# Softmax exponentials of a windowed attention: one instruction per group or one per head, and their place in the first block

## Chip, core and metric

The kernel runs on one core of a Trainium2 chip. The metric is the device time of one execution in microseconds (us). Engines: PE (TensorE) multiplies matrices, with its weight loads shown apart as PEld; DVE (VectorE) and ACT (ScalarE) do elementwise work; POOL (GpSimd) a little of it; SP (SyncE) issues the DMAs. An engine takes its instructions in the order in which they are written.

## What is computed

A windowed attention with 8 memory keys, then two MLPs with different gates, all in float32 from outside:

```python
for c in range(nc):                        # chunks of 32 queries, 16 keys to the left, 8 to the right
    k_full = np.concatenate([mem_k, k_ctx], axis=2)
    v_full = np.concatenate([mem_v, v_ctx], axis=2)
    scores = scale * np.matmul(q_c, k_full.transpose(0, 1, 3, 2))
    scores = scores - np.max(scores, axis=-1, keepdims=True)
    a = np.exp(scores)
    a = a / (np.sum(a, axis=-1, keepdims=True) + 1e-09)
    out[:, :, c_start:c_end] = np.matmul(a, v_full)
x = out as 3072 tokens x 512               # 4 batches x 768, 8 heads x 64
h = x @ w_in;  g = h - np.tanh(h);  x = g @ w_out          # first MLP, d_ff 2048
h = x @ w_in2; g = piecewise quadratic gate of h; x = g @ w_out2
```

## The kernel before

**Attention.** 24 groups `t` of 4 chunks each hold 128 queries, 8 heads and a window of 64 keys, so a group's scores are a 128 x 512 tile: per query row 8 heads of 64 scores. A group runs through these steps, each of which is a function:
- `att_scores` (L320): 128 small matmuls write the scores into one PSUM pair of banks, `a`.
- `att_max` (L338, L340): DVE takes each head's maximum from PSUM (one reduction), then subtracts it in two instructions that write the SBUF tile `e`.
- `att_exp` (L350): ACT takes the exponential of the whole of `e` in place, one 128 x 512 instruction.
- `att_sum` (L354 to L356): DVE sums each head's exponentials, adds 1e-9 and takes reciprocals.
- `att_transpose` (L362): four PE transposes of `e` into PSUM; `att_at` (L367): ACT copies them out; `att_values` (L376): 128 small matmuls; `att_norm` (L386): DVE multiplies by the reciprocals; `att_x` (L396): four PE transposes; `att_xh` and `att_xl` (L402, L407): ACT and DVE split the result in a high and a low part, the input `xh`, `xl` of the first MLP.

**First MLP.** Six blocks of 512 tokens (four groups each), 16 steps a block. Step `s`: `hidden(s)` (L472) is 12 matmuls into one of two PSUM banks `h`; `gate(s)` has an ACT tanh (L482) and a DVE subtraction (L483), called the gate end here; 16 steps later `output` (L507) multiplies. Weights are rounded on the way: `round_act` (L133 `raw`, L136 `stage`, ACT), `round_mag` and `round_sign` (L142, L143, L151, DVE; L156, POOL), then split in two parts `whi` (L168, ACT) and `wlo` (L175, DVE).

**Order.** Everything is written out by hand. The start runs the groups 0 to 3 one after the other: each pass `j` is scores, maximum, exponential, transposes, copy, values, norm, transposes, split, and PE's gaps are filled with matmuls on zeros (`warm`, L941). In the start ACT's `raw` (L133) stands between the exponential and the copy `at`. Then a loop over steps `i` runs, in this order, lists of events: `before`, `rounds` (weight rounding), then `hidden(i + 1)`, `gate(i + 1)`, then `behind`, then `output`. The groups 4 to 8 are spread over the steps 0, 3, 6, 9, 12 of block 0, where there is no `output` yet; the groups 9 to 23 come every fourth step. For a group at step `i` scores and maximum stand in `behind` of step `i`, exponential and sum in `behind` of `i + 1`, so behind the tanh of `hidden(i + 2)`; the transposes (`slot_b`) follow `hidden(i + 2)` for groups up to 8, and stand behind `hidden(i + 3)` for later ones. Up to group 7 the transposes write a PSUM pair of their own; from group 8 on (`t > 2 * PER - 1`, L434) they write the pair in which the scores stood. The second MLP follows from about 577 us on and has no part in the change.

Of the kernel before, what the change touches and what calls it, by code (L numbers as in the profile page):

```python
# [8 lines left out]
F32 = mybir.dt.float32  # L9
# [4 lines left out]
AF = mybir.ActivationFunctionType  # L14
ALU = mybir.AluOpType
AX = mybir.AxisListType
# [12 lines left out]
WIN = NMEM + LEFT + CHUNK + SEEN  # L29
# [9 lines left out]
PER = 4  # L39
# [34 lines left out]
def tile_memory_attention_two_mlps(  # L74
# [9 lines left out]
    nc = tc.nc  # L84
# [7 lines left out]
    att = ctx.enter_context(tc.tile_pool(name="att", bufs=2))  # L92
# [7 lines left out]
    def slot(tag, name, dtype=F32):  # L100
        return slots.tile([128, 512], dtype, tag=tag, name=name)
# [62 lines left out]
    def split_weights_hi(s, which):  # L164
        phase, b, fc = steps[s]
        r = raw_t[phase, which, fc]
        hi = slot(f"whi{which}_{s % (W1O if which else 2)}", f"whi{which}_{s}", F32R)
        nc.scalar.activation(out=hi, in_=r, func=AF.Copy)  # L168
        split_t[s, which] = hi

    def split_weights_lo(s, which):
        phase, b, fc = steps[s]
        r, hi = raw_t[phase, which, fc], split_t[s, which]
        lo = slot(f"wlo{which}_{s % (W1O if which else 2)}", f"wlo{which}_{s}", F32R)
        nc.vector.tensor_tensor(out=lo, in0=r, in1=hi.bitcast(F32), op=ALU.subtract)  # L175
        split_t[s, which] = hi, lo
# [8 lines left out]
    def w1o_store(s):  # L185
        for i, t in enumerate(split_t[s, 1]):
            nc.sync.dma_start(out=w1o_d[steps[s][2]][:, i, :], in_=t.bitcast(F32))

    def w1o_load(s):
        if s < NS:  # L190
            t = [slot(f"w{w}1_{s % W1O}", f"w{w}1_{s}", F32R) for w in ("hi", "lo")]
            for i in range(2):
                nc.sync.dma_start(out=t[i].bitcast(F32), in_=w1o_d[steps[s][2]][:, i, :])
            split_t[s, 1] = t
# [60 lines left out]
    st = {}  # L255
# [54 lines left out]
    scale = 1.0 / float(D) ** 0.5  # L310
# [17 lines left out]
    def att_max(t):  # L328

        e = slots.tile([128, 4, 2, WIN], F32, tag=f"e{t % 2}", name=f"e{t}")  # L330
        mx = att.tile([128, 2, NPAIR], F32, tag="mx", name=f"mx{t}")
        s = st[t]["sp"]

        if t % GPB == 0:
            nc.vector.memset(s[:CHUNK, :, :, NMEM:NMEM + LEFT], NEG)
        if t % GPB == GPB - 1:
            nc.vector.memset(s[128 - CHUNK:, :, :, WIN - SEEN:], NEG)
        nc.vector.tensor_reduce(out=mx, in_=s, op=ALU.max, axis=AX.X)  # L338
        for hh in range(2):
            nc.vector.tensor_tensor(  # L340
                out=e.rearrange("p (b c) u k -> p c u b k", c=2)[:, hh],
                in0=s[:, hh].rearrange("p (u b) k -> p u b k", u=2),
                in1=mx[:, hh].rearrange("p (u b) -> p u b", u=2)[:, :, :, None].to_broadcast([128, 2, 2, WIN]),
                op=ALU.subtract,
            )
        st[t]["e"] = e

    def att_exp(t):
        e = st[t]["e"]
        nc.scalar.activation(out=e, in_=e, func=AF.Exp, scale=scale)  # L350

    def att_sum(t):
        r = att.tile([128, 4, 2], F32, tag="r", name=f"r{t}")
        nc.vector.tensor_reduce(out=r, in_=st[t]["e"], op=ALU.add, axis=AX.X)  # L354
        nc.vector.tensor_scalar(out=r, in0=r, scalar1=1e-9, scalar2=None, op0=ALU.add)
        nc.vector.reciprocal(out=r, in_=r)  # L356
        st[t]["r"] = r

    def att_transpose(t, p):
        e = st[t]["e"].rearrange("p g u k -> p g (u k)")  # L360
# [56 lines left out]
    def slot_s(t):  # L417
        if t < NG:
            att_scores(t, st_pair.pop(t))
            att_max(t)  # L420
# [7 lines left out]
    def slot_exp(t):  # L428
        att_exp(t)
        att_sum(t)  # L430
# [18 lines left out]
    def x_tiles(phase, b):  # L449
        if (phase, b) not in x_t:  # L450
            x_t[phase, b] = tuple(
                xsp.tile([128, KC, N], F32R, tag=f"x{w}{b % 2}", name=f"x{w}_{b}") for w in "hl"
            )
        return x_t[phase, b]
# [7 lines left out]
    def hidden(s, n0=0, n1=N, parts=range(3)):  # L462
        phase, b, fc = steps[s]
        xh, xl = x_tiles(phase, b)
        hi, lo = split_t[s, 0]
        if s not in h_t:
            h_t[s] = ps_h.tile([128, 512], F32, tag="h", name=f"h{s}")[:, :N]
        hp = h_t[s][:, n0:n1]
        for j in parts:
            w, x = ((hi, xh), (hi, xl), (lo, xh))[j]  # L470
            for kc in range(KC):
                nc.tensor.matmul(  # L472
                    hp, w[:, kc * 128:(kc + 1) * 128], x[:, kc, n0:n1],
                    start=j == 0 and kc == 0, stop=j == 2 and kc == KC - 1,
                )

    def gate(s):
        phase, b, fc = steps[s]
        hp = h_t[s]
        g = slot(f"g{fc}", f"g{s}")  # L480
        g_t[s] = g
        nc.scalar.activation(out=g, in_=hp, func=AF.Tanh)  # L482
        nc.vector.tensor_tensor(out=g, in0=hp, in1=g, op=ALU.subtract)  # L483
        h_t.pop(s)

    def split_g(s):
        hi, lo = slot(f"ghi{s % GSETS}", f"ghi{s}", F32R), slot(f"glo{s % GSETS}", f"glo{s}", F32R)
        split_to(g_t[s], hi, lo)
        g_t[s] = hi, lo
# [350 lines left out]
    for n, p in enumerate(PAIRS[PREP_FIRST:]):  # L840
        f = [
            (prep_act, *p), (prep_rest, *p, 0), (prep_rest, *p, 1), (prep_sums, *p),
            (prep_split, *p, 0), (prep_split, *p, 1), (prep_split, *p, 2), (prep_split, *p, 3),
        ]
# [26 lines left out]
        w1o_load(s + W1O)  # L871


    before, rounds, behind = {}, {}, {}

    def at_step(events, i, f, *args):
        assert i >= 0
        events.setdefault(int(i), []).append((i, f, args))


    for t in range(PER, NG + 1):
        k = t - PER
        i = SPACE_A[0] * min(k, PER) + SPACE_A[1] * max(0, k - PER)

        at_step(behind, max(0, i - 1 + 0.3) if k <= PER else i, slot_v, t)
        at_step(behind, max(0, i - 1 + 0.4) if k <= PER else i + 0.2, slot_norm, t)
        at_step(behind, i + 0.1, slot_s, t)
        if t < NG:
            at_step(behind, i + 1, slot_exp, t)

        at_step(before if k <= PER else behind, i + 2, slot_b, t)
        at_step(before, i + 1.01, att_load, t + 2, True, False)
        if t - 1 >= PER:
            at_step(before, (i if k <= PER else i + 1) + 0.02, att_load, t + 1, False, True)
    at_step(before, 0.5, att_load, PER + 1)
    for w in range(2):
        for fc in range(FC):
            p = fc - EARLY + w * (FC + 2)
# [6 lines left out]
    for n, pair in enumerate(PAIRS):  # L905
        p = int(PREP + PREP_EVERY * n)
# [41 lines left out]
    for j in range(PER):  # L948
        w = 0, 0, j
        pool, tag = ((ps_a, "a"), (ps_acc, "acc0"))[j % 2]  # L950
# [11 lines left out]
        else:  # L962
            warm(KEEP["s"], t_ps)
        att_max(j)
        att_exp(j)
        round_act(*w, 0)
        if 1 <= j <= 2:
            split_weights_lo(j - 1, 0)
        att_sum(j)
        att_transpose(j, t_ps)  # L970
        att_at(j)
# [29 lines left out]
    def run(events, i):  # L1001
        for _, f, args in sorted(events.pop(i, []), key=lambda e: e[0]):
            f(*args)

    for i in range(-1, NS - 1):
        o = i - LAG
        if 0 <= i and i + 2 < NS:
            split_weights_hi(i + 2, 0)
            split_weights_lo(i + 2, 0)
        if 0 <= o + 1:  # L1010
            split_g(o + 1)
            if o + 1 < FC:
                split_weights_hi(o + 1, 1)
                split_weights_lo(o + 1, 1)
        if 0 <= o < FC:
            w1o_store(o)
        if o + W1O - 2 >= FC:
            w1o_load(o + W1O - 2)
        run(before, i)
        run(rounds, i)  # L1020
        hidden(i + 1, EARLY_N if i + 1 < 2 else 0)
        gate(i + 1)
        run(behind, i)
        if o >= 0:
            output(o)
# [11 lines left out]
    for e in plan:  # L1037
# [6 lines left out]
        if e[0] == "P" and e[1] == 0 and e[3] in (1, 4, 2, 7):  # L1044
# [2 lines left out]
            events += 1  # L1047
            if events == 8 * (len(PAIRS) - PREP_FIRST) + 2:
                spare.extend(f"prep{i}" for i in range(9))
    assert not before and not rounds and not behind  # L1050


# [46 lines left out]
```

## Time and profile before

| | |
|---|---|
| median of 3 runs | 1085.6 us (1085.06 to 1085.8) |
| the profiled execution | 1086.91 us |
| its span, first to last instruction | 1085.1 us |
| PE busy | 1065.2 us, 98% |
| DVE / ACT busy | 794.2 us, 73% / 614.7 us, 57% |
| PE busy from 0 to 43 us (the start) | 31.53 of 43 us |
| PE busy from 43 to 110 us (block 0) | 62.71 of 67 us |
| PE busy from 110 to 580 us (blocks 1 to 5) | 470.00 of 470 us |
| granted PE clock over the span | 0.998 of full speed |

One core has one span, and its last instruction ends the time. PE is busy nearly always, so a change in ACT's or DVE's work shows in the time only where PE waits for it, and the rows by stretch say where PE has gaps. A clock of 1 is 2.4 GHz, 0.50 is 1.2 GHz.

### The profile page before, as it was taken

To read this page: it belongs to the slowest core of one execution; us is meant where nothing else is said; L and a number is where in the kernel's file an instruction comes from. 1 tells how busy PE (TensorE), PEld (TensorE's weight loads), DVE (VectorE), ACT (ScalarE), POOL (GpSimd) and SP (SyncE) were. 2 spreads that over 40 slices of the span, in tenths; PEclk is the share of its full clock that TensorE was granted. 3 is DMA by queue.
4 is the path that set the end of the run, shared out by engine and by line. 5 is a ranking of instruction groups with operands and counts; after the bars stand their busy time and mean duration, and the time that the engine had idled before them with its cause. 6 is when DMAs were issued, how large, how long until landed. Compare 5 with 4: busy or idle time off the path is not lost.

```text
span 1085.1 us, 20769 instructions
## 1 busy us (share of the span) xinstructions
PE 1065.2 (98%) x7655; PEld 870.1 (80%) x7655; DVE 794.2 (73%) x1397; ACT 614.7 (57%) x1085; POOL 42.5 (4%) x38
## 2 busy tenths in 40 slices
PE   7899999999999999999999999999999999999998
PEld 3677888888888888888888888878888888888886
DVE  4699987787777777868885765698367797467854
ACT  3566665545454544545465645757477766477553
POOL 1132222000000000000000000000000000000000
PEclk9999999999999999999999999999999999999999
DMA  9997885888788788658779875677766777766664
GB/s 213 242 260 208 263 243 166 256 278 255 246 266 274 223 258 261 224 182 271 275 251 325 293 244 170 199 268 221 240 192 194 233 251 226 220 194 194 203 203 146
DMA packets 201316, 253.04 MB, mean 233 GB/s; under 512 B 65024, under 2 KB 114176, under 8 KB 201216
## 3 DMA queue, kind: packets, MB, share of 16 engines
q1 hardware_dynamic: 201216, 251.72, 75.9%
q8 instruction: 61, 1.00, 0.4%
q14 instruction: 39, 0.32, 0.1%
HBM read 201.33 MB, written 50.33 MB: 232 GB/s over the span
## 4 chain that ended last, share of the span: by engine, by line
PE 97%; ACT 1%; DVE 1%; issue 0%; ACTq 0%; DVEq 0%
PE h L472 25%; PE acc L507 24%; PE acc L793 21%; PE qa L706 12%; PE qc L706 6%; PE qb L706 3%; PE a L376 1%; PE a L320 1%; PE start_tx L941 1%; PE b L362 1%; PE b L396 1%; ACT e L350 0%; PE start_a L320 0%; PE start_a L376 0%; PE start_tx L396 0%
## 5 line engine op out<-in xcount | busy, mean ns | idle before, releaser
L482 ACT ACTIVATE g<-h 128x512 f32<-128x512 f32 x96 | 57.3, 597 | 222.6 <-PE h L472 207.6
L793 PE MATMUL acc<-ghi,inG 128*128 128x512 f32 x672 | 183.1, 389 | 0.0
L222 DVE TENSOR_TENSOR glo<-g,ghi 128x512 fp32r<-128x512 f32 x206 | 140.2, 687 | 35.8 <-ACT ghi L221 34.9
L221 ACT ACTIVATE ghi<-g 128x512 fp32r<-128x512 f32 x206 | 127.4, 626 | 46.5 <-PE acc L793 23.7
L793 PEld LDWEIGHTS acc<-ghi,inG 128*128 128x128 f32 x672 | 126.1, 188 | 26.2
L706 PE MATMUL qa<-xc,inP 128*128 128x512 f32 x576 | 140.1, 389 | 0.0
L483 DVE TENSOR_TENSOR g<-h,g 128x512 f32<-128x512 f32 x96 | 66.2, 690 | 82.0 <-ACT g L482 81.2
L706 PEld LDWEIGHTS qa<-xc,inP 128*128 128x128 f32 x576 | 108.1, 188 | 22.4
L507 PE MATMUL acc<-ghi,whi 128*128 128x512 f32 x384 | 109.2, 399 | 0.0
L793 PE MATMUL acc<-glo,inG 128*128 128x512 f32 x336 | 107.2, 390 | 0.4 <-DVE glo L222 0.3
L472 PE MATMUL h<-xl,whi 128*128 128x512 f32 (+2 forms) x392 | 104.5, 388 | 1.6 <-issue 1.6
L507 PE MATMUL acc<-ghi,wlo 128*128 128x512 f32 x384 | 105.7, 390 | 0.0
L507 PE MATMUL acc<-glo,whi 128*128 128x512 f32 x384 | 105.7, 389 | 0.0
L472 PE MATMUL h<-xh,whi 128*128 128x512 f32 (+2 forms) x392 | 105.2, 390 | 0.0
L472 PE MATMUL h<-xh,wlo 128*128 128x512 f32 (+2 forms) x392 | 104.3, 388 | 0.0
L648 ACT ACTIVATE t<-g,half 128x512 f32<-128x512 f32 x72 | 52.2, 725 | 82.2 <-DVE g L644 82.2
L472 PEld LDWEIGHTS h<-xl,whi 128*128 128x128 f32 x392 | 73.4, 189 | 16.9 <-issue 1.9
L472 PEld LDWEIGHTS h<-xh,wlo 128*128 128x128 f32 x392 | 73.5, 189 | 14.7
L507 PEld LDWEIGHTS acc<-ghi,wlo 128*128 128x128 f32 x384 | 72.1, 188 | 15.4
L507 PEld LDWEIGHTS acc<-glo,whi 128*128 128x128 f32 x384 | 72.1, 188 | 15.2
L472 PEld LDWEIGHTS h<-xh,whi 128*128 128x128 f32 x392 | 72.1, 188 | 14.5
L175 DVE TENSOR_TENSOR wlo<-raw,whi 128x512 fp32r<-128x512 f32 x112 | 79.6, 710 | 4.7 <-ACT whi L168 4.7
(108 smaller groups left out, 1522.3 us busy)
## 6 DMA issues: line engine op xcount, KB each, us to landing
inP<-part SPq DMA_DIRECT2D x168, 256.0 KB, 2.9
inG<-part SPq DMA_DIRECT2D x168, 256.0 KB, 2.9
whi<-w1o SPq DMA_DIRECT2D x80, 256.0 KB, 4.3
wlo<-w1o SPq DMA_DIRECT2D x80, 256.0 KB, 4.5
stage<-w_in SPq DMA_DIRECT2D x32, 512.0 KB, 5.4
stage<-w_out SPq DMA_DIRECT2D x32, 512.0 KB, 4.5
part<-preph SPq DMA_DIRECT2D x64, 256.0 KB, 4.4
part<-prepl SPq DMA_DIRECT2D x48, 256.0 KB, 4.3
```

The costliest lines, as they stand in the source:

```text
L175: nc.vector.tensor_tensor(out=lo, in0=r, in1=hi.bitcast(F32), op=ALU.subtract)
L221: nc.scalar.activation(out=hi, in_=src, func=AF.Copy)
L222: nc.vector.tensor_tensor(out=lo, in0=src, in1=hi.bitcast(F32), op=ALU.subtract)
L320: nc.tensor.matmul(sp[j * CHUNK:(j + 1) * CHUNK, hh, pr, :], qt[j][hh * D:(hh + 1) * D, pr, :], kt[j][hh * D:(hh + 1) * D, pr, :], start=T ...
L362: nc.tensor.transpose(p[:, g * GQ:(g + 1) * GQ], e[:, g, :], ident)
L472: nc.tensor.matmul(hp, w[:, kc * 128:(kc + 1) * 128], x[:, kc, n0:n1], start=j == 0 and kc == 0, stop=j == 2 and kc == KC - 1,)
L482: nc.scalar.activation(out=g, in_=hp, func=AF.Tanh)
L483: nc.vector.tensor_tensor(out=g, in0=hp, in1=g, op=ALU.subtract)
L507: nc.tensor.matmul(acc_t[dm], w[:, dm * 128:(dm + 1) * 128], g, start=first and j == 0, stop=last and j == 2,)
L648: nc.scalar.activation(out=t, in_=h, func=AF.Relu, scale=0.5, bias=half)
L706: nc.tensor.matmul(o, w[:, k * 128:(k + 1) * 128], z[k], start=i in (1, 2, 5) and j == 0 and k == 0, stop=j == 2 and k == 1, skip_group_ch ...
L793: nc.tensor.matmul(bank[a][c], w[:, c * 128:(c + 1) * 128], g, start=first and j == 0, stop=last and j == 2, skip_group_check=True,)
```

## The change

- DVE no longer subtracts the maximum. It multiplies the 8 maxima by -scale (one 128 x 8 instruction).
- ACT takes the exponentials from the scores in PSUM, head by head: 8 instructions of 128 x 64 with the negated maximum as a bias operand, each of which also hands out the sum of its exponentials (`accum_out`). In the built program a second short ACT instruction stands behind each of the 8, which writes that sum.
- DVE's sum over `e` is gone; the 1e-9 and the reciprocal stay.
- For the groups 4 to 8 the maximum moves ahead of the gate end of the same step on DVE (a new list `between`), and the exponentials move into `rounds`, ahead of the next tanh on ACT.

```diff
-        for hh in range(2):
-            nc.vector.tensor_tensor(
-                out=e.rearrange("p (b c) u k -> p c u b k", c=2)[:, hh],
-                in0=s[:, hh].rearrange("p (u b) k -> p u b k", u=2),
-                in1=mx[:, hh].rearrange("p (u b) -> p u b", u=2)[:, :, :, None].to_broadcast([128, 2, 2, WIN]),
-                op=ALU.subtract,
-            )
-        st[t]["e"] = e
+        nc.vector.tensor_scalar(out=mx, in0=mx, scalar1=-scale, scalar2=None, op0=ALU.mult)
+        st[t]["e"], st[t]["mx"] = e, mx
 
     def att_exp(t):
-        e = st[t]["e"]
-        nc.scalar.activation(out=e, in_=e, func=AF.Exp, scale=scale)
+        e, mx, s = (st[t][x] for x in ("e", "mx", "sp"))
+        st[t]["r"] = r = att.tile([128, 4, 2], F32, tag="r", name=f"r{t}")
+        for g in range(4):
+            for u in range(2):
+                hh, pr = g % 2, 2 * u + g // 2
+                nc.scalar.activation(
+                    out=e[:, g, u, :], in_=s[:, hh, pr, :], func=AF.Exp, scale=scale,
+                    bias=mx[:, hh, pr:pr + 1], accum_out=r[:, g, u:u + 1],
+                )
...
-        nc.vector.tensor_reduce(out=r, in_=st[t]["e"], op=ALU.add, axis=AX.X)
...
-        at_step(behind, max(0, i - 1 + 0.3) if k <= PER else i, slot_v, t)
+        at_step(behind if k else between, max(0, i - 1 + 0.3) if k <= PER else i, slot_v, t)
...
-        at_step(behind, i + 0.1, slot_s, t)
+        at_step(between if k <= PER else behind, i + 0.1, slot_s, t)
         if t < NG:
-            at_step(behind, i + 1, slot_exp, t)
+            at_step(rounds if k <= PER else behind, i + 1.5 if k <= PER else i + 1, slot_exp, t)
...
         hidden(i + 1, EARLY_N if i + 1 < 2 else 0)
+        run(between, i)
         gate(i + 1)
         run(behind, i)
```

ACT's queue around group 5's exponentials in block 0, before (`g<-h` is a tanh, `e` the exponentials, `whi`, `raw`, `stage` weight rounding, `at` and `xh` copies from PSUM; the numbers behind a name only tell buffers apart):

```order
L136 ACTIVATE stage_8_780<-stage_8_780 128x512
L482 ACTIVATE g_990<-h_977 128x512
L350 ACTIVATE e_951<-e_951 128x512
L168 ACTIVATE whi_7_998<-raw_7_889 128x512
L402 ACTIVATE xh_1011<-b_1002 128x4x128
L367 ACTIVATE at_1014<-b_1002 128x512
```

And the same place after the change:

```order
L136 ACTIVATE stage_8_799<-stage_8_799 128x512
L348 ACTIVATE e_973,r_1001<-a_875,mx_974 128x64 x8
L481 ACTIVATE g_1025<-h_1012 128x512
L168 ACTIVATE whi_7_1028<-raw_7_914 128x512
L401 ACTIVATE xh_1041<-b_1032 128x4x128
L366 ACTIVATE at_1044<-b_1032 128x512
```

The eight exponentials, which read the scores `a` and the maxima `mx`, moved in front of the tanh; the copies stay behind it.

DVE's queue for the same group, before (`L338` is the maximum, `L340` the subtractions, `L483` a gate end):

```order
L151 SCALAR_TENSOR_TENSOR raw_7_889<-stage_7_702,raw_7_889 128x512
L483 TENSOR_TENSOR g_916<-h_903,g_916 128x512
L337 MEMSET a_850 32x2x4x8
L338 TENSOR_REDUCE mx_952<-a_850 128x8
L340 TENSOR_TENSOR e_951<-a_850,mx_952 128x2x2x64 x2
L175 TENSOR_TENSOR wlo_6_959<-raw_6_825,whi_6_957 128x512
```

And after:

```order
L151 SCALAR_TENSOR_TENSOR raw_7_914<-stage_7_722,raw_7_914 128x512
L337 MEMSET a_875 32x2x4x8
L338 TENSOR_REDUCE mx_974<-a_875 128x8
L339 TENSOR_SCALAR mx_974<-mx_974 128x8
L482 TENSOR_TENSOR g_978<-h_928,g_978 128x512
L175 TENSOR_TENSOR wlo_6_983<-raw_6_850,whi_6_981 128x512
```

The maximum moved in front of the gate end, and a 128 x 8 instruction stands where the two subtractions stood.

PE's queue at the transposes of group 8 with what they wait for, before (a name ending in _49 is the semaphore of that engine):

```order
L396 MATMUL b_1554<-ident,xn_1450 128x128 [waits DVE_49,PE_49]
L396 MATMUL b_1554<-ident,xn_1450 128x128 x3
L362 MATMUL b_1554<-ident,e_1511 128x128 [waits Activation_49]
L362 MATMUL b_1554<-ident,e_1511 128x128 x3
```

And after:

```order
L395 MATMUL b_1599<-ident,xn_1490 128x128 [waits DVE_49,Activation_49]
L395 MATMUL b_1599<-ident,xn_1490 128x128 x3
L361 MATMUL b_1599<-ident,e_1548 128x128 x4
```

The wait for ACT moved from the second four transposes to the first four, which write the banks that the exponentials now read.

## Rows read from the trace of the kernel before

**Rows 1.** The page's first part: busy time, share, instructions of each engine

```profile
PE 1065.2 (98%) x7655; PEld 870.1 (80%) x7655; DVE 794.2 (73%) x1397; ACT 614.7 (57%) x1085; POOL 42.5 (4%) x38
```

**Rows 2.** Who PE waited for: us in total, times, longest us

```profile
PE b L362 <- ACT e L350: 4.3, 5, 1.2
PE start_tx L362 <- ACT e L350: 3.4, 3, 1.4
```

**Rows 3.** Timeline, pass 0 of the start: start us, us, engine line, names [idle before]

```profile
7.68 0.69 DVE L338 TENSOR_REDUCE mx<-start_a 128x8 f32<-128x512 f32 x1
8.41 0.76 DVE L340 TENSOR_TENSOR e<-start_a,mx 128x256 f32<-128x256 f32 x2
9.20 0.63 ACT L350 ACTIVATE e<-e 128x512 f32<-128x512 f32 x1 [6.97 <-DVE e L340]
9.73 0.67 ACT L133 ACTIVATE raw<-stage 128x512 f32<-128x512 f32 x1
...
9.97 0.63 PE L362 MATMUL start_tx<-ident,e 128*128 128x128 f32 x4 [1.39 <-ACT e L350]
...
10.58 0.17 DVE L355 TENSOR_SCALAR r<-r 128x8 f32<-128x8 f32 x1
10.63 0.60 ACT L367 ACTIVATE at<-start_tx 128x512 f32<-128x512 f32 x1 [0.23 <-PE start_tx L362]
...
11.28 0.59 PE L941 MATMUL start_tx<-zeros 128*128 128x512 bf16 x2 [0.69 <-ACT at L367]
```

**Rows 4.** Timeline, pass 3 of the start

```profile
40.80 1.33 PE L472 MATMUL h<-xl,whi 128*128 128x384 f32 x3 [1.61 <-issue]
41.92 1.05 PE L396 MATMUL start_tx<-ident,xn 128*128 128x128 f32 x4
```

**Rows 5.** PE in half-microsecond stretches: us, PE busy (x), PEclk, DMA share, GB/s

```profile
40.50:41.00 0.50, 0.20 (x1) 0.73 0.17 38
...
44.00:44.50 0.50, 0.50 (x6) 0.86 0.27 47
```

**Rows 6.** Timeline, group 4 in block 0

```profile
49.33 0.66 ACT L136 ACTIVATE stage<-stage 128x512 int32<-128x512 uint32 x1
...
52.26 1.17 PE L472 MATMUL h<-xh,whi 128*128 128x512 f32 x4
```

**Rows 7.** Timeline, group 5 in block 0

```profile
59.80 0.69 DVE L151 SCALAR_TENSOR_TENSOR raw<-stage,raw 128x512 int32<-128x512 int32 x1
...
60.62 0.67 ACT L136 ACTIVATE stage<-stage 128x512 int32<-128x512 uint32 x1
...
62.58 0.60 PE L396 MATMUL b<-ident,xn 128*128 128x128 f32 x4
...
64.36 1.17 PE L472 MATMUL h<-xh,whi 128*128 128x512 f32 x4
```

**Rows 8.** Timeline, group 8 in block 0

```profile
95.19 0.86 PE L320 MATMUL a<-k,q 64*32 64x64 f32 x64
...
98.84 0.60 PE L396 MATMUL b<-ident,xn 128*128 128x128 f32 x4
...
100.62 1.17 PE L472 MATMUL h<-xh,whi 128*128 128x512 f32 x4
```

**Rows 9.** Groups of ACT instructions, shapes apart: x count, busy us, mean ns, idle before

```profile
L648 ACT ACTIVATE t<-qa,half 128x512 f32<-128x512 f32 x24 | 16.1, 673 | 0.0
L221 ACT ACTIVATE preph<-raw 128x256 fp32r<-128x256 f32 x32 | 12.3, 408 | 0.0
...
L221 ACT ACTIVATE preph<-raw 128x512 fp32r<-128x512 f32 x8 | 5.0, 623 | 0.0
...
L108 ACT ACTIVATE unused<-half 128x1 f32<-128x1 f32 x1 | 0.2, 203 | 0.0
```

**Rows 10.** Timeline, group 9 in block 1

```profile
118.06 0.63 ACT L350 ACTIVATE e<-e 128x512 f32<-128x512 f32 x1
...
121.51 0.60 PE L396 MATMUL b<-ident,xn 128*128 128x128 f32 x4
```

More of the change, by code (lines that the diff above doesn't have):

```diff
@@ L338, in att_max @@
         nc.vector.tensor_reduce(out=mx, in_=s, op=ALU.max, axis=AX.X)
-        for hh in range(2):
-            nc.vector.tensor_tensor(
-                out=e.rearrange("p (b c) u k -> p c u b k", c=2)[:, hh],
-                in0=s[:, hh].rearrange("p (u b) k -> p u b k", u=2),
-                in1=mx[:, hh].rearrange("p (u b) -> p u b", u=2)[:, :, :, None].to_broadcast([128, 2, 2, WIN]),
-                op=ALU.subtract,
-            )
-        st[t]["e"] = e
-    def att_exp(t):
-        e = st[t]["e"]
-        nc.scalar.activation(out=e, in_=e, func=AF.Exp, scale=scale)
+        nc.vector.tensor_scalar(out=mx, in0=mx, scalar1=-scale, scalar2=None, op0=ALU.mult)
+        st[t]["e"], st[t]["mx"] = e, mx
+    def att_exp(t):
+        e, mx, s = (st[t][x] for x in ("e", "mx", "sp"))
[7 more added lines that the diff above has]
+                )
     def att_sum(t):
-        r = att.tile([128, 4, 2], F32, tag="r", name=f"r{t}")
-        nc.vector.tensor_reduce(out=r, in_=st[t]["e"], op=ALU.add, axis=AX.X)
+        r = st[t]["r"]
         nc.vector.tensor_scalar(out=r, in0=r, scalar1=1e-9, scalar2=None, op0=ALU.add)
         nc.vector.reciprocal(out=r, in_=r)
-        st[t]["r"] = r
     def att_transpose(t, p):
@@ L871, in older @@
         w1o_load(s + W1O)
-    before, rounds, behind = {}, {}, {}
+    before, rounds, between, behind = {}, {}, {}, {}
     def at_step(events, i, f, *args):
@@ L1049, in tile_memory_attention_two_mlps @@
                 spare.extend(f"prep{i}" for i in range(9))
-    assert not before and not rounds and not behind
+    assert not before and not rounds and not between and not behind
 def _windows(np, mem, x):
```

## The prediction

> **What bounds the kernel now.** First the page's busy shares: PE is busy for 98% of the span, DVE and ACT for 73% and 57% [rows 1]. So removing DVE work is worth nothing by itself; only PE's gaps can give or take time. Second, whom PE waits for [rows 2]: the largest item is the exponential. Five transposes in block 0 wait 4.3 us for it together, one for each of the groups 4 to 8, and three in the start wait 3.4 us. The reader is to see that both places of the change lie on a chain that ends in PE, and that 4.3 us is the most that moving block 0's exponentials can give back. Third, the timeline of one pass of the start [rows 3]: maximum, subtractions, exponential, transposes, copy follow each other with gaps of 0.03 to 0.23 us. PE waits 1.39 us in it although zeros are multiplied to fill gaps. The start is a chain of latencies; what is added to a link there is added to the time. In blocks 1 to 5 PE has no gap at all.
>
> **What one group's exponentials cost after the change.** Before, from the maximum's end (7.68 + 0.69 = 8.37) to the end of the exponential (9.20 + 0.63 = 9.83) it is 1.46 us: two subtractions on DVE, one instruction on ACT [rows 3]. After, the negation comes first: 0.04 us behind the maximum, like the first subtraction, 0.17 long, like another 128 x 8 instruction, and 0.03 to ACT, so 0.24 us [rows 3]. Then come eight exponentials of 64 columns.
> - One of them, estimated: the row that reads PSUM and takes a bias from a tile, as the new form does, is 673 ns for 512 columns. From 256 to 512 columns a copy grows from 408 to 623 ns, 0.84 ns a column, so 448 columns less make 0.30 us [rows 9].
> - Next to each other: `raw` began at 9.73, 0.10 before the exponential ended [rows 3]; independent ACT instructions overlap by 0.10.
> - The short instruction that writes the sum has no row. From below it is hidden in the overlap and costs nothing: a spacing of 0.20 us. From above it is a whole ACT instruction that overlaps nothing, 0.20 us by the 128 x 1 row [rows 9], with 0.03 on both sides: a spacing of 0.56. I take 0.30 + 0.20 - 0.10 = **0.40 us**, because it must wait for its own exponential but not the next exponential for it.
>
> Eight at 0.40 make 7 x 0.40 + 0.30 + 0.20 = 3.30 us (1.70 at the lower end, 4.45 at the upper).
>
> The Trainium skill ("ScalarE: Activation LUTs", section What ACT_TABLE_LOAD costs) gives 280 ns + 0.833 ns a column with a bias from a tile and 93 ns of overlap, so 0.24 us of spacing, and prices no accumulator; by it the whole change would come out near nothing. The 408, 623 and 673 ns rows agree with its slope; no row here shows the sum's cost.
>
> **The start, passes 0 to 2.** The last exponential ends at 8.37 + 0.24 + 3.30 = 11.91 in pass 0. The transposes wait for their own head pairs, so only the last is late. But `raw` (0.67 us) stands between the exponentials and the copy `at` on ACT. Before, it was hidden behind the transposes; now that cover is gone: `at` starts at 11.91 - 0.10 + 0.67 - 0.10 = 12.38 instead of 10.63, **1.75 us** later (0.15 and 2.9 at the ends), and the rest of the pass hangs on it. DVE's saved 0.7 us of sum hides nothing, since the reciprocals are due much later, with the values. Three passes: **5.25 us** (0.45 to 8.7).
>
> **Pass 3.** Behind its values PE idles 1.61 us for nothing that the profile shows [rows 4]. If that is a fixed arrival, such as its own instructions, the 1.75 us fall into it and 0.15 is left; if not, all 1.75 count. I take **0.15**.
>
> **Block 0.** ACT can begin the exponentials when the step's `stage` is done, earlier than before by the wait for the hidden matmuls and the tanh; DVE's maximum must also be there. The next hidden matmuls follow the last exponential by some 0.25 us, a wait of 0.05 to 0.14 and one of the four transposes that take 0.6.
> - Group 4: `stage` ends at 49.99; 50.02 + 3.30 + 0.25 = 53.57, against 52.26 before [rows 6]: **+1.3** (-0.3 to +2.5).
> - Groups 5 to 7, alike: from 61.19, where `stage` ends less the overlap, to 61.2 + 3.30 + 0.25 = 64.75, against 64.36 [rows 7]: +0.4 each, **+1.2** (-1.7 to +4.6). At the lower end the `xn` transposes, which end at 63.18, and four more of 0.6 set the end, 63.78. DVE's round sign ended at 60.49 [rows 7]; that is 0.4 too late for a maximum and negation by 61.2, but the 0.7 us sum that stood ahead of it in the queue is gone. If it doesn't help, 1.2 us more.
> - Group 8: no weight rounding is left on ACT, so only the scores (end 96.05) count: exponentials from 97.0 to 100.3. Now the `xn` transposes wait too, since they write the banks that the exponentials read: eight of 0.15 and 0.14 of wait, 101.64 against 100.62 [rows 8]: **+1.0** (-0.6 to +2.2).
>
> Together +3.5. What is queued behind the exponentials on ACT: the tanh, then `whi` and the copies. The tanh of group 5's step comes some 1.7 us late; its gate end frees a bank that is wanted only two steps later, and no PE matmul waits for it sooner. On DVE the reciprocal now waits for the sums with the gate end behind it, under the same cover.
>
> **Blocks 1 to 5.** The exponentials stay behind the tanh and PE needs them much later: in group 9, the tightest, 121.51 - 118.06 = 3.45 us after they begin [rows 10]. 3.30 fits; the upper end would add 1.0. Cost **0**. DVE's 2 us less a group meet no wait of PE.
>
> **The clock.** PE's clock fell from 2.4 to 1.2 GHz once, between 40.5 and 44.5 us [rows 5], right behind the 1.61 us of idle; four transposes took 1.05 us in it against 0.63 at the full clock [rows 3, 4]. Gaps of 1.39 and 0.69 us with transposes between them did not bring that about [rows 3]. After the change those two gaps become one of about 4 us with four single transposes in it, in each of three passes. I count one more fall: at most half of those 3.5 us, nothing if PE is not the late one there; **1.2 us**, nearer the top since most of PE's work there is on the chain. "TensorE: Matmul & The Clock Gate" of the Trainium skill (section HAM oscillation) has the same rule, that gaps in PE's work put its clock back; it speaks against this change, and the 40.5 us row agrees.
>
> **Sum.** 5.25 + 0.15 + 3.5 + 1.2 = 10.1 us. The profiled execution took 1086.91 us, 1.8 more than its span and 1.3 more than the median; the sum is of differences within it, so I add it to the median: 1085.6 + 10.1 = **1095.7 us**.
>
> **Rivals.**
> - The sum is free (spacing 0.20). For it: ACT overlaps what is independent. Against: a readout depends on its exponential. Then 0.45 - 0.3 - 1.7 - 0.6 = -2.2: the exponentials ahead of tanh win most of block 0's waits and the start hardly pays, 1083.4 us, **faster**. It decides from a spacing of about 0.25 down. Chance 0.15.
> - The readout half overlaps (0.30): 2.85 + 0.1 + 0.5 - 1.2 + 0.2 = +2.5, without a fall of the clock: 1088 us. Chance 0.17.
> - The readout overlaps nothing (0.56): 8.7 + 1.3 + 2.5 + 4.6 + 2.2 + 1.0 = +20, 1106 us; or the clock falls in all three passes at 0.40: 8.9 + 3.6 = 1098 us, and more if each costs 1.7. Together chance 0.18, most of it at 1098 to 1102.
> - The order does not move: against it stand ACT's and DVE's queues, where it has moved. No chance.
>
> **How the numbers follow.** The forecast (spacings of 0.35 to 0.45, with none to two falls of the clock: 1092 to 1097.5) has 0.50. The range, **1084.5 to 1101.5**, leaves out most of the free readout and the slowest cases. This kernel can be told from no change by about 0.2%, 2.2 us: faster, below 1083.4, gets 0.11; the rest of the free case and half of the half-overlapped one make 0.13 for the same; slower 0.76.
>
> **What would show it.** Right: the exponentials 0.4 us apart, `at` in pass 0 about 1.7 us later behind the maximum, PE's wait for exponentials in block 0 grown from 4.3 to about 8 us, and blocks 1 to 5 as long as before. Wrong: exponentials 0.2 us apart, or PE's wait in block 0 below 2 us; and if `at` doesn't wait for `raw`, or the clock in the start stays at one, the term of that name falls.

## The result and the profile after

The changed kernel takes **1091.47 us** in the median of 6 runs (1090.43 to 1092.93), the kernel before beside it 1085.48 (1085.06 to 1086.3): a ratio of 1.0057, 95% interval 1.0046 to 1.0068. It is slower by 6.0 us; 10.1 were forecast. The profiled execution of the changed kernel took 1090.43 us with a span of 1088.6, the fastest of its runs, while the profiled execution of before, 1086.91, lies above its runs here. The two traces therefore differ by only 3.5 us, and what is read from one pair of profiles has to be weighed against the medians.

The page's line of busy times answers to [rows 1]. VectorE (DVE) and ScalarE (ACT) have changed as meant: DVE loses 23 us, ACT gains 43. PE, at 98% in both, still decides. The second line is the clock that was granted to PE in 40 slices of 27 us, in tenths of full speed (9 is 90% or more): the first two, which hold the start and the beginning of block 0, are the only ones below 9.

```profile
PE 1070.6 (98%) x7649; PEld 871.6 (80%) x7655; DVE 771.1 (71%) x1349; ACT 657.6 (60%) x1445; POOL 42.6 (4%) x38
PEclk8899999999999999999999999999999999999999
```

Where the time came from is seen when both spans are cut at the same two instructions, the scores of group 4 and those of group 9. The columns are the stretch, its length, PE's busy time (instructions), the granted clock, the share of the DMA engines, GB/s. Before:

```profile
0.00:46.82 46.82, 35.35 (x640) 0.96 0.90 221
46.82:109.69 62.87, 58.58 (x869) 1.00 0.93 241
109.69:1085.10 975.41, 971.23 (x6163) 1.00 0.75 233
```

After:

```profile
0.00:50.70 50.70, 39.50 (x633) 0.83 0.86 212
50.70:113.39 62.69, 59.89 (x870) 1.00 0.95 234
113.39:1088.60 975.21, 971.23 (x6169) 1.00 0.75 233
```

The start is 3.88 us longer, block 0 (groups 4 to 8) 0.18 shorter, and all that follows 0.2 shorter. The start's clock has gone from 0.96 to 0.83.

**The exponentials.** The timeline of pass 0 after answers to [rows 3] (start, duration, engine and line, operation, names, idle time before it with what ended it):

```profile
7.60 0.69 DVE L338 TENSOR_REDUCE mx<-start_a 128x8 f32<-128x512 f32 x1
8.33 0.17 DVE L339 TENSOR_SCALAR mx<-mx 128x8 f32<-128x8 f32 x1
8.60 0.31 ACT L348 ACTIVATE e<-start_a,mx 128x64 f32<-128x64 f32 x1 [6.37 <-PE start_tx L940]
8.81 0.19 ACT L348 ACTIVATION_READ_ACCUMULATOR e<-start_a,mx 128x1 f32 x1
8.90 0.30 ACT L348 ACTIVATE e<-start_a,mx 128x64 f32<-128x64 f32 x1
...
9.44 0.30 PE L361 MATMUL start_tx<-ident,e 128*128 128x128 f32 x1 [0.95 <-ACT e L348]
...
10.84 0.24 ACT L348 ACTIVATION_READ_ACCUMULATOR e<-start_a,mx 128x1 f32 x1
10.93 0.70 ACT L133 ACTIVATE raw<-stage 128x512 f32<-128x512 f32 x1
...
11.13 0.33 PE L361 MATMUL start_tx<-ident,e 128*128 128x128 f32 x1 [0.26 <-ACT e L348]
...
11.50 0.62 ACT L366 ACTIVATE at<-start_tx 128x512 f32<-128x512 f32 x1
```

Each sum is an instruction of its own, ACTIVATION_READ_ACCUMULATOR, some 0.2 us long. It begins 0.2 us behind its exponential, and the next exponential 0.09 us behind the readout's beginning: the spacing is 0.29 us (8.60, 8.90, 9.19 and on to 10.64), not 0.40. From the maximum's end to the copy `at` it is 11.50 - 8.29 = 3.21 us, against 10.63 - 8.37 = 2.26 before: **0.95 us** later, not 1.75. `raw` does stand between the last exponential and `at`, as the prediction said, but the last transpose ends only at 11.13 + 0.33 = 11.46, and `at` follows it by 0.04 us, much as before (9.97 + 0.63 = 10.60, then 10.63). So `raw` delayed `at` by nothing that the trace can tell from the transposes.

**Who PE waits for** (total, times, longest) answers to [rows 2]:

```profile
PE start_tx L361 <- ACT e L348: 3.7, 11, 0.9
PE b L361 <- ACT e L348: 2.2, 7, 0.7
...
PE b L395 <- ACT e L348: 0.6, 1, 0.6
```

In block 0 the wait fell from 4.3 to 2.2 + 0.6 = 2.8 us, where it was to grow to about 8. But the time hardly fell: the transposes of `e` in block 0 now start one by one as their head pairs come, and their own busy time grew. PE's windows for that line alone, before and after:

```profile
46.82:109.69 62.87, 3.28 (x20) 1.00 0.93 241
```

```profile
50.70:113.39 62.69, 4.69 (x20) 1.00 0.95 234
```

PE was idle for 62.87 - 58.58 = 4.29 us of block 0, and is for 62.69 - 59.89 = 2.80; it was busy for 58.58 and is for 59.89. So 1.49 us of waiting gave way to 1.31 us of work, nearly all of it this line's (4.69 - 3.28 = 1.41). A transpose by itself counts 0.33 us; four in a row take 0.60 to 0.66 together.

**The clock.** PE in windows of a microsecond, after. Before there was one fall, from 40.9 to 44.3 us [rows 5]:

```profile
20.00:21.00 1.00, 0.66 (x2) 0.97 0.97 346
21.00:22.00 1.00, 0.35 (x1) 0.50 1.03 278
...
31.00:32.00 1.00, 0.74 (x4) 0.91 1.32 243
...
34.00:35.00 1.00, 0.92 (x65) 0.80 0.98 318
...
41.00:42.00 1.00, 1.00 (x6) 0.79 0.93 227
```

Now there are two, from 21.0 to 31.2 and from 34.6 to 41.4 us, 17 us at 1.2 GHz where there were 3.4. Passes 1 and 2 lie in them and take 2.05 and 2.57 us longer than before (from scores to scores: 16.20 to 27.64 and on to 38.80, against 15.42, 24.81 and 33.40). Pass 0, at the full clock, ends 0.78 later, and pass 3 takes 1.52 less: the 1.61 us of idle time of [rows 4] and the fall behind it aren't there. Together that is the 3.88 of the start.

### The profile page after: what moved, and what is told of

Read it like the earlier page. It is cut to its first block, busy times and chain, and to the rows that moved or that the text cites. A ratio compares the mean times of both kernels' runs of the same rounds, so it can differ in the third digit from the quotient of the medians.

```text
span 1088.6 us, 21098 instructions
## 1 busy us (share of the span) xinstructions
PE 1070.6 (98%) x7649; PEld 871.6 (80%) x7655; DVE 771.1 (71%) x1349; ACT 657.6 (60%) x1445; POOL 42.6 (4%) x38
## 4 chain that ended last, share of the span: by engine, by line
PE 93%; ACT 3%; DVE 2%; DMA 1%; issue 0%; SPq 0%; ACTq 0%; DVEq 0%
PE acc L506 24%; PE h L471 22%; PE acc L792 20%; PE qa L705 12%; PE qc L705 6%; PE qb L705 3%; ACT e L348 2%; PE a L375 1%; PE a L320 1%; PE b L361 1%; PE b L395 1%; PE start_tx L940 1%; DVE mx L338 1%; PE start_a L320 0%; DMA start<-qkv_t 0%
## 5 line engine op out<-in xcount | busy, mean ns | idle before, releaser
L175 DVE TENSOR_TENSOR wlo<-raw,whi 128x512 fp32r<-128x512 f32 x112 | 82.6, 738 | 5.6 <-ACT whi L168 4.7
```

## Experiments

All runs are compared with runs of the kernel before on the same chip, whose median was 1085.94 us beside fill, start_old, no_accum and order_only, 1085.3 beside heads_old_order, neg_on_act, before_fewer_zeros and old_start_filled, and 1086.03 beside the last two. "Start" ends with the scores of group 4, "block 0" runs from there to the scores of group 9; both are from one profile each, with the clock granted in it.

| kernel | median us (range, runs) | ratio to before (95%) | start, clock | block 0, clock |
|---|---|---|---|---|
| before | 1085.48 (1085.06-1086.3, 6) | 1 | 46.82, 0.96 | 62.87, 1.00 |
| after | 1091.47 (1090.43-1092.93, 6) | 1.0057 (1.0046-1.0068) | 50.70, 0.83 | 62.69, 1.00 |
| fill | 1089.33 (1088.44-1090.51, 6) | 1.0027 (1.0016-1.0038) | 47.04, 1.00 | 64.10, 0.97 |
| start_old | 1086.65 (1083.41-1087.93, 12) | 0.9999 (0.9989-1.0009) | 46.44, 0.93 | 64.18, 0.97 |
| no_accum | 1087.41 (1085.91-1089.21, 11) | 1.0011 (0.9999-1.0022) | 46.96, 0.89 | 63.72, 1.00 |
| heads_old_order | 1101.18 (1100.49-1105.0, 4) | 1.0147 (1.0119-1.0175) | 50.62, 0.87 | 72.79, 0.98 |
| order_only | 1086.52 (1084.87-1088.15, 12) | 1.0004 (0.9995-1.0013) | 46.58, 0.96 | 64.09, 1.00 |
| neg_on_act | 1089.6 (1087.86-1092.74, 12) | 1.0039 (1.0024-1.0054) | 51.66, 0.80 | 62.26, 1.00 |
| before_fewer_zeros | 1088.61 (1087.02-1091.34, 12) | 1.0026 (1.0012-1.004) | 49.72, 0.73 | 62.82, 1.00 |
| before_more_zeros | 1085.9 (1083.6-1087.72, 11) | 0.9994 (0.9983-1.0004) | 46.83, 0.96 | 63.11, 1.00 |
| old_start_filled | 1084.3 (1082.83-1087.32, 12) | 0.9988 (0.9974-1.0002) | 44.55, 1.00 | 62.25, 1.00 |
| old_start_filled_again | 1084.89 (1083.26-1087.85, 11) | 0.9991 (0.9982-1.0001) | 45.03, 1.00 | 62.45, 1.00 |

The theory: the instructions that read out the sums ("readouts") lengthen the start's chain, and the longer gaps bring PE's clock down, which costs as much again. The rivals: the exponentials alone cost the time and the clock is a by-product; or block 0 costs it.

**fill** takes the clock's falls away from the changed kernel, by two multiplications of zeros behind each of the first three transposes in passes 0 to 2:

```diff
+FILL = 2
...
+            if spare_ps is not None and g < 3:
+                warm(FILL, spare_ps)
...
-        att_transpose(j, t_ps)
+        att_transpose(j, t_ps, None if last else x_ps)
```

> The changed kernel with two multiplications of zeros behind each of the first three transposes of the start's passes 0 to 2, into a bank that holds nothing yet. If the clock's falls in the start are what the longer chain costs beside its own length, they go: granted clock of the start at 1.00 up to pass 3, and 2.5 to 4 us less than the changed kernel, 1087.5 to 1089. If the fall costs nothing because the chain waits for ACT and DVE anyway: 1091.5 as before, whatever the clock.

The start now runs at the full clock and is 3.66 us shorter, though PE has more instructions in it:

```profile
0.00:47.04 47.04, 38.31 (x657) 1.00 0.91 227
47.04:111.14 64.10, 61.35 (x870) 0.97 0.87 230
```

Pass by pass, the scores of passes 1 to 3 begin here, and then in the changed kernel, at:

```profile
16.39 0.86 PE L321 MATMUL start_a<-start,start 64*32 64x64 f32 x64
25.87 0.86 PE L321 MATMUL start_a<-start,start 64*32 64x64 f32 x64
35.37 0.86 PE L321 MATMUL start_a<-starty,start 64*32 64x64 f32 x64
```

```profile
16.20 0.86 PE L320 MATMUL start_a<-start,start 64*32 64x64 f32 x64
27.64 1.18 PE L320 MATMUL start_a<-start,start 64*32 64x64 f32 x64
38.80 1.19 PE L320 MATMUL start_a<-starty,start 64*32 64x64 f32 x64
```

So the passes 1 and 2 take 9.48 and 9.50 us at the full clock, and 11.44 and 11.16 with the falls: these cost 3.62 us. Pass 2 took 8.59 before, so the chain by itself is 0.91 longer, as the 0.95 of pass 0 says.

The ratio falls from 1.0057 to 1.0027, so the falls in the start cost about half of the loss, 0.30% or 3.3 us (2.6 by the medians), and the rest stands without them. The median of 1089.33 lies a little above the expected 1087.5 to 1089. Not foreseen: in this profile the clock falls in block 0, at group 4's transposes, from 53.3 to 56.7 us, which the profile of the changed kernel doesn't show. Two of the six runs had a clock of 1.0 over the whole span; they took 1088.4 and 1088.7 us. The kernel before, which has falls of its own, also had two such runs beside them, of 1084.6 and 1084.7. By these few runs the change costs about 4 us with no fall on either side, and about 2 of the 6.0 us are what its falls cost beyond those that were there before.

**start_old** does one part alone: groups 0 to 3 keep the subtractions, one exponential and DVE's sum (`if t < PER`), and groups 4 on are as changed:

```diff
-        nc.vector.tensor_scalar(out=mx, in0=mx, scalar1=-scale, scalar2=None, op0=ALU.mult)
+        if t < PER:
+            for hh in range(2):
+                nc.vector.tensor_tensor(
...
+        else:
+            nc.vector.tensor_scalar(out=mx, in0=mx, scalar1=-scale, scalar2=None, op0=ALU.mult)
...
+        if t < PER:
+            nc.scalar.activation(out=e, in_=e, func=AF.Exp, scale=scale)
+            return
...
+        if t < PER:
+            nc.vector.tensor_reduce(out=r, in_=st[t]["e"], op=ALU.add, axis=AX.X)
```

> Groups 0 to 3 in the old form (subtraction on DVE, one exponential, sum on DVE), groups 4 to 23 as in the changed kernel, order of block 0 as in the changed kernel. If the loss is all in the start: 1084.5 to 1086, level with the kernel before. If block 0 or the later blocks pay a share: 1087 to 1089.

The ratio is 0.9999 (the median of 1086.65 lies between the two expected ranges): with the start undone, the loss is gone, to within 0.1%. The runs spread with the clock, from 1083.41 us (clock 1.0) to 1087.93 (0.995). So the loss is the start's, and block 0 doesn't cost it. Block 0 is 1.3 us longer in this profile, which has a fall of the clock there as fill has.

**no_accum** takes the sums back to DVE and leaves the eight exponentials everywhere:

```diff
-                    bias=mx[:, hh, pr:pr + 1], accum_out=r[:, g, u:u + 1],
+                    bias=mx[:, hh, pr:pr + 1],
...
+        nc.vector.tensor_reduce(out=r, in_=st[t]["e"], op=ALU.add, axis=AX.X)
```

> The changed kernel without the accumulator output: ACT takes the eight exponentials, DVE sums them as before. If each readout adds the 0.1 us that the trace of the changed kernel shows between exponentials (0.29 apart), they stand 0.20 us apart here, a group's are done 0.75 us earlier, and the start's three passes and what hangs on them are 2 to 3 us shorter: 1088 to 1089.5. If readouts hide in ACT's own gaps: 1091 to 1092, and up to 0.7 us a group in block 0 for DVE's sum.

It measures the disputed price directly. In the timeline of pass 0 the eight are shown as one run, with the maximum ahead of them and the copy `at` behind:

```profile
7.89 0.69 DVE L338 TENSOR_REDUCE mx<-start_a 128x8 f32<-128x512 f32 x1
...
8.89 1.74 ACT L348 ACTIVATE e<-start_a,mx 128x64 f32<-128x64 f32 x8 [6.67 <-DVE mx L339]
...
11.05 0.62 ACT L367 ACTIVATE at<-start_tx 128x512 f32<-128x512 f32 x1
```

1.74 us for eight is a spacing of (1.74 - 0.31) / 7 = 0.20. So a readout adds 0.09 to 0.10 us to each exponential, 0.7 to a group. From the maximum's end to `at` it is 11.05 - 8.58 = 2.47 us: of the 0.95 by which `at` comes later in the changed kernel, 0.74 are the readouts' and 0.21 the rest of the change's. The Trainium skill ("ScalarE: Activation LUTs", section What ACT_TABLE_LOAD costs) would give 0.24 of spacing without a sum; the measured one is shorter. The time of 1087.41 us lies below the expected 1088 to 1089.5: the start is 3.74 us shorter than in the changed kernel, with less of the clock lost (0.89 against 0.83), while block 0, with DVE's sum back, is 1.03 longer. How much of the 4 us against the changed kernel is due to the clock wasn't separated.

**heads_old_order** takes the other part away: the changed exponentials, but in block 0 the maxima behind the gate ends and the exponentials behind the tanh, as before:

```diff
-        at_step(behind if k else between, max(0, i - 1 + 0.3) if k <= PER else i, slot_v, t)
+        at_step(behind, max(0, i - 1 + 0.3) if k <= PER else i, slot_v, t)
...
-        at_step(between if k <= PER else behind, i + 0.1, slot_s, t)
+        at_step(behind, i + 0.1, slot_s, t)
...
-            at_step(rounds if k <= PER else behind, i + 1.5 if k <= PER else i + 1, slot_exp, t)
+            at_step(behind, i + 1, slot_exp, t)
```

> The changed kernel with block 0 in the old order: exponentials by head, but behind the tanh, and the maxima behind the gate ends. If the new order is what pays for the 2.4 us that a group's exponentials now take, block 0 loses 1.2 to 1.5 us in each of the groups 4 to 7 and over 2 us in group 8 against the kernel before, and the whole comes out 6 to 9 us above the changed kernel, 1097 to 1100.5. If the order moves nothing, as in the run with the order alone: 1091.5.

Block 0 takes 10 us longer: 1.5 in each of the groups 5 to 7 and 2.2 in group 8, much as expected, but 3.1 in group 4, where the clock falls from 57.5 to 60.9 us. The median of 1101.18 lies just above the expected range. PE's waits for the exponentials are 7.0 + 3.1 us, where the prediction had put about 8 with the new order:

```profile
PE b L361 <- ACT e L348: 7.0, 16, 1.3
...
PE b L395 <- ACT e L348: 3.1, 1, 3.1
```

**order_only** is the reverse: the kernel before with the new order, but subtractions, exponential and sum in their old form. Against the kernel before it holds the three `at_step` lines just shown, the other way round, and:

```diff
+        run(between, i)
         gate(i + 1)
```

> The kernel before with nothing but the new order in block 0: maximum and subtractions ahead of the gate end, the one whole exponential ahead of the tanh. If the exponential's place behind the tanh is what PE waits for in block 0, its wait falls from 4.3 us to about 1.5 and the time to about 1082.5 to 1083.5. If the maxima come too late on DVE for the move to matter: 1085 to 1086.

This one missed. PE waits less for exponentials in block 0 (1.5 us in place of 4.3), but a wait that wasn't there takes their place: group scores wait for a PSUM bank until `xn` is read out of it. Two of its waits:

```profile
PE a L320 <- DVE xn L386: 3.0, 4, 0.9
...
PE b L362 <- ACT e L350: 1.5, 3, 0.6
```

DVE works there without a gap, and part of its lateness is seen in one small instruction on the way, the addition of 1e-9 (L355) behind the sum. With the sum ahead of the gate end it begins while an addition of POOL runs, and ends with it. Group 5 here, and then in the kernel before, where the same addition begins later:

```profile
65.38 1.31 POOL L156 TENSOR_TENSOR raw<-raw,stage 128x512 int32<-128x512 int32 x1 [3.13 <-DVE raw L151]
...
65.88 0.85 DVE L355 TENSOR_SCALAR r<-r 128x8 f32<-128x8 f32 x1
```

```profile
65.06 1.32 POOL L156 TENSOR_TENSOR raw<-raw,stage 128x512 int32<-128x512 int32 x1 [3.12 <-DVE raw L151]
...
66.16 0.26 DVE L355 TENSOR_SCALAR r<-r 128x8 f32<-128x8 f32 x1
```

It takes 0.84 or 0.85 us in each of the groups 4 to 7, against 0.25 or 0.26 before, so DVE loses 0.59 us a group; the 3.0 us of waits are 0.3 to 0.9 a group. No run has the new order without this, so what the order alone would be worth stays open.

So neither half of the change gained by itself, and the eight exponentials are bearable in block 0 only in the new order.

**neg_on_act** follows a row that nothing had announced, another small instruction that ends with POOL's. Group 4 after, on DVE, POOL and ACT; it answers to [rows 6]:

```profile
52.83 0.69 DVE L338 TENSOR_REDUCE mx<-a 128x8 f32<-128x512 f32 x1
53.05 1.31 POOL L156 TENSOR_TENSOR raw<-raw,stage 128x512 int32<-128x512 int32 x1 [4.81 <-DVE raw L151]
...
53.55 0.84 DVE L339 TENSOR_SCALAR mx<-mx 128x8 f32<-128x8 f32 x1
...
54.51 0.32 ACT L348 ACTIVATE e<-a,mx 128x64 f32<-128x64 f32 x1 [0.64 <-DVE mx L339]
```

The negation of eight numbers, 0.17 us elsewhere, takes 0.84 here and ends with POOL's addition (53.05 + 1.31 = 54.36; 53.55 + 0.84 = 54.39). In groups 6 and 7 it takes 0.48 and 0.71, again to POOL's end. In group 5, where no addition of POOL runs beside it, it takes 0.17. Here ACT puts the negation ahead of its exponentials:

```diff
-        nc.vector.tensor_scalar(out=mx, in0=mx, scalar1=-scale, scalar2=None, op0=ALU.mult)
+        nc.scalar.activation(out=mx, in_=mx, func=AF.Copy, scale=-scale)
```

> The changed kernel with the negation of the maxima on ACT, in front of the exponentials, instead of DVE. In the changed kernel's trace the negation took 0.84, 0.48 and 0.71 us in groups 4, 6 and 7, and ended with POOL's addition each time; it took 0.17 elsewhere. If DVE waits there for POOL, the wait goes: exponentials start 0.4 to 0.7 us earlier in these groups, block 0 is 1 to 1.5 us shorter, and fewer falls of the clock begin in group 4: 1089 to 1090.5. If the maximum itself was late: 1091.5.

It takes 0.19 us on ACT and waits for nobody, though POOL's addition runs beside it (54.01 to 55.33):

```profile
54.01 1.32 POOL L156 TENSOR_TENSOR raw<-raw,stage 128x512 int32<-128x512 int32 x1 [4.83 <-DVE raw L151]
...
54.73 0.19 ACT L344 ACTIVATE mx<-mx 128x8 f32<-128x8 f32 x1
```

Block 0 is 0.43 us shorter than in the changed kernel, not the expected 1 to 1.5. The median of 1089.6 lies in the expected range and 1.9 below the changed kernel's, but the ranges overlap and so do the intervals, and the start is 0.96 longer in this profile; what the wait costs is read from block 0.

**before_fewer_zeros** is the opposite of fill: the kernel before with fewer zeros in the start's gaps (`KEEP` of 2, 2, 1, 1 in place of 5, 2, 3, 2), so that only the clock is disturbed:

```diff
-KEEP = {"s": 5, "t": 2, "v": 3, "x": 2}
+KEEP = {"s": 2, "t": 2, "v": 1, "x": 1}
```

> The kernel before with 2, 1 and 1 instead of 5, 3 and 2 multiplications of zeros behind scores, values and transposes of the start's passes. Nothing on the chain is longer; only PE does less in its gaps. If falls of the clock cost time by themselves: granted clock 0.985 to 0.992 and 2 to 5 us more than the kernel before, 1088 to 1091. If the chain waits for ACT and DVE anyway, 1085 to 1086 at the same lower clock.

The start's clock was 0.73 and the kernel 0.26% slower, 2.8 us, with no instruction added and the same chain. The clock alone can thus cost time. As for the size: a clock of 0.73 over 49.72 us is some 27 us at 1.2 GHz, 23 more than before. At that price the 13.6 us that the changed kernel has more than before would cost 1.6, near the 2 us that are left when the kernel before is charged for its own falls.

**old_start_filled** joins what had helped: the old form in groups 0 to 3 with `KEEP["s"]` of 9, the changed heads and order behind it with the negation on ACT, and two multiplications of zeros ahead of each of group 4's transposes. Beside the diffs of start_old and neg_on_act it has:

```diff
-KEEP = {"s": 5, "t": 2, "v": 3, "x": 2}
+KEEP = {"s": 9, "t": 2, "v": 3, "x": 2}
...
+            if spare_ps is not None:
+                warm(2, spare_ps)
...
-            att_transpose(t, pair[:, 1, :])
+            att_transpose(t, pair[:, 1, :], tx[PER - 1][:, 0, :] if t == PER else None)
```

> Meant to beat both: groups 0 to 3 in the old form with 9 instead of 5 multiplications of zeros behind the scores, groups 4 to 23 by head with the negation on ACT and the new order, and two multiplications of zeros in front of each of group 4's transposes. If the falls of the clock and POOL's lock are what the other runs lost: granted clock 0.999 or above, block 0 about 62 us long, and 1082.5 to 1084. If more zeros delay the chain instead: 1085 to 1087.

It came to 1084.3 us, 0.3 above the expected range, and the interval of its ratio (0.9974 to 1.0002) includes no change. Both the start and block 0 are at the full clock in its profile:

```profile
0.00:44.55 44.55, 35.59 (x645) 1.00 0.97 238
44.55:106.80 62.25, 60.74 (x877) 1.00 0.88 239
```

**before_more_zeros** and **old_start_filled_again** ask side by side whether its 0.12% comes from the zeros or from the change: the first is the kernel before with the `KEEP` line just shown and nothing else.

> The kernel before with nine instead of five zero multiplications ahead of the first copy of each pass of the start, as in old_start_filled, and nothing of the change. If those zeros alone bring what old_start_filled brought: about as fast as that, 1083.5 to 1084.5 us, with no fall of PE's clock in the start. If block 0's exponentials by ScalarE in the new order bring something of their own (62.25 against 62.87 us of block 0): 0.5 us or so slower than it, 1084.5 to 1085.5 us.

> The kernel of old_start_filled beside before_more_zeros on the same chip: 1083 to 1084.5 us again. If the change of the heads is worth nothing beside the zeros, the two are equal within 0.1%; if it is worth its 0.6 us of block 0, this one is the faster by that.

Both lie within 0.1% of before, the first at 0.9994 (0.9983 to 1.0004), the second at 0.9991 (0.9982 to 1.0001), and both medians lie 0.4 us above what was expected. In the profiles block 0 is 0.66 us shorter (62.45 against 63.11), and PE's waits for exponentials there are 0.8 + 0.5 us, while before_more_zeros keeps the 4.3 of the kernel before. Two lines of its waits also show that nine zeros don't keep the start free of idle time: 2.2 us of it are for nothing that the profile shows.

```profile
PE b L362 <- ACT e L350: 4.3, 5, 1.2
PE start_a L376 <- issue: 2.2, 1, 2.2
```

A gain of the change in groups 4 on, of about 0.6 us, is what the profiles point to, but the times of these runs can't tell it from none. No version was shown to be faster than the kernel before.

## Why the prediction was right, and where its terms were not

Slower was right, and 1091.47 lies in the range of 1084.5 to 1101.5, 4.2 us below the forecast. That the sum came so near is in part luck: the chain and block 0 were put some 6 us too high, the clock some 2 us too low, and the range is 17 us wide. Of the four signs of being right that the prediction named, only the last, blocks 1 to 5, came as stated; the spacing, the delay of `at` and PE's wait in block 0 did not. The terms:

- **Spacing, 0.40 us: mis-sized; it is 0.29.** The step that failed is "it must wait for its own exponential but not the next exponential for it", from which the sum became 0.30 + 0.20 - 0.10. The trace has the readout begin 0.1 us before its exponential has ended, and the next exponential 0.09 behind the readout's beginning: both overlap. The rival with 0.30 had the size.
- **The start, 1.75 a pass: right place, too long.** With seven spacings of 0.29 the same steps give 8.37 + 0.24 + 7 x 0.29 + 0.30 + 0.20 = 11.14 for the last readout's end and 11.14 - 0.10 + 0.67 - 0.10 = 11.61 for `at`: 0.98 later, and the trace shows 0.95. That `raw` is what holds `at` isn't shown, since the last transpose ends at the same time. Three passes are some 2.9 us in place of 5.25. The profiles at the full clock agree roughly: 47.04 us in fill against 44.55 and 45.03 in old_start_filled.
- **Pass 3, +0.15: the rows fit.** The 1.61 us of idle time were taken for a fixed arrival, and they are missing in the profile of the changed kernel. Counted in the traces, such idle time stands at one place: behind the 604th weight load of PE, in five profiles (before, order_only, before_more_zeros, old_start_filled, old_start_filled_again), 0.6 to 2.25 us long, and it ends between 38.95 and 41.55 us. With 12 zeros more ahead of it, as in the last three, it moves from L472 by 12 matmuls, into the values. The kernels that come to that load at 41.25 us or later (start_old, fill, no_accum, the changed kernel and the rest) show no such gap there. A shorter one, of 0.4 to 1.0 us, stands behind the 222nd load in before, order_only and start_old. What arrives isn't shown, and its time varies between executions, so the size of the term can't be had from one profile.
- **Block 0, +3.5: wrong sign, measured -0.2.** Mostly this is the spacing again. For group 5, 61.2 + 2.5 + 0.25 = 63.95, 0.4 before the 64.36 of [rows 7], and from scores to the next hidden matmuls the trace shows 0.58, 0.31 and 0.30 less in groups 5 to 7 (before 5.43 each). The exponentials of group 5 do start when `stage` ends less the overlap, as the step said:

```profile
65.50 0.67 ACT L136 ACTIVATE stage<-stage 128x512 int32<-128x512 uint32 x1
66.06 0.31 ACT L348 ACTIVATE e<-a,mx 128x64 f32<-128x64 f32 x1
```

  Group 4 was put at +1.3 and took 1.0 more, but for another reason: 0.67 us of it are the negation's wait for POOL, which had no term. Group 8 was put at +1.0 and took 0.16 less. The wait that was named for it, of the `xn` transposes for the banks that the exponentials read, did come, 0.58 us long; with the shorter spacing it was less than what the new order gave:

```profile
103.50 0.66 PE L395 MATMUL b<-ident,xn 128*128 128x128 f32 x4 [0.58 <-ACT e L348]
```

- **Blocks 1 to 5, 0: right.** 975.41 us before, 975.21 after.
- **The clock, +1.2: too small, about 3.3 against fill, about 2 against a kernel before that is charged for its own falls.** The mechanism was right (one fall more, in the start, behind the longer gaps), and the trace agrees in direction with the rule of the Trainium skill that was weighed for it ("TensorE: Matmul & The Clock Gate", section HAM oscillation): 17 us at 1.2 GHz against 3.4. The step that failed is "at most half of those 3.5 us": the falls lasted 10.2 and 6.8 us, not 3.5. PE paused for 0.2 to 0.7 us four times in the first and twice in the second, while before it was busy without a pause through the whole fall; that the pauses drew the falls out fits, but no run separates it.

Seen from here, the right case was on the page but in two pieces: 1088 us for the spacing of 0.30 without a fall of the clock, and a fall counted only with 0.40. fill's two runs at the full clock took 1088.4 and 1088.7 us, and 1088 with the 3.3 for the clock makes 1091.3. The rival's sum of 2.5 is only partly confirmed by that, because it too had 0.5 - 1.2 + 0.2 for block 0 and fill's block 0 held a fall of its own in the profile.

## What to carry to other kernels

Splitting one wide ACTIVATE into eight to save VectorE work lost time here where PE waited for the result at once, and gained nothing that the times could show elsewhere. Price it by the spacing in a trace, and with a summed output count a second instruction. On a chain that ends in PE, price the clock together with the chain: in this case longer gaps came with longer stays at half the clock, and these were a third to a half of the loss. And a tiny instruction on the way to the critical engine should be looked at for what runs beside it, not only for its own length.

## What the runs showed of the hardware

- A summed output of ACT is a second instruction of 0.19 to 0.25 us that overlaps both neighbours, and costs 0.09 to 0.10 us net for a 128 x 64 exponential from PSUM (0.29 us of spacing against 0.20).
- VectorE's 128 x 8 multiplication from SBUF to SBUF lasted until GpSimd's addition ended, in all four places of the changed kernel where it began during one (0.84, 0.48, 0.71 and, in group 9, 0.23 us, against 0.17 in the other 20), while the reduction ahead of it, which reads PSUM, kept its 0.69. The Trainium skill ("SBUF — State Buffer", section Who interferes with whom) says that VectorE in a two-port mode, which a tensor_scalar can enter, and GpSimd contend for a shared pair of ports: whoever issues first gets it for the whole instruction, and the other is blocked. The trace agrees: the negation ends 0.02 to 0.04 us behind POOL's addition. On ACT the same negation took 0.19 us beside the same addition.
- The 128 x 8 addition of 1e-9 does the same: 0.84 to 0.85 us in groups 4 to 7 of order_only and 0.61 in group 9 of the changed kernel, each time to 0.02 to 0.04 us behind POOL's end.
- Group 4's four single transposes, with gaps of some 0.26 us between them, had a fall of the clock to 1.2 GHz at or within a microsecond behind them in fill, start_old and heads_old_order, and none in the changed kernel and in neg_on_act. With zeros ahead of the transposes (old_start_filled) block 0 was at the full clock in both profiles. What decides between them was not tested.
